# Rounding attention values on GpSimd, and one MLP tile's low parts on VectorE

## The chip, the cores and the metric

The kernel runs on one core of a Trainium2 chip. The metric is the device time of one execution in microseconds (us); before the change the median of three runs is 1063.71 us. A core has TensorE (PE in the rows, its weight loads are PEld), VectorE (DVE), ScalarE (ACT), GpSimd (POOL) and SyncE (SP), which issues the DMAs. Each engine works through its own list of instructions in order and waits on semaphores for the others.

## The reference, cut to what matters

Causal attention with an added memory read-out, and then two MLPs, one after the other, over the 2304 rows that the attention leaves:

```python
# q, k, v: 4 batches x 8 heads x 576 rows x 64
a = softmax(causal(q @ k.T / 8));  local = a @ v
mem = (phi(q) @ M_prev) / (phi(q) . z_prev + 1e-6)
x = g * mem + (1 - g) * local          # g = sigmoid(beta), per head; x: 2304 x 512
h = x @ w_in;   x = elu(h) @ w_out     # w_in 512 x 2048, w_out 2048 x 512
h = x @ w2_in;  y = max(0.01 * h, h) @ w2_out
```

The weights come as 64-bit floats, which the kernel takes apart into words and turns into float32 itself.

## The kernel before, in words

**Precision.** Most matmuls use operands of type fp32r. A float32 value is written as two such numbers: the rounded value (the high part) and the difference between the value and it (the low part). A product then takes three matmuls (high x high, low x high, high x low). Rounding is a copy into a tile of that type; the low part is a `tensor_tensor` subtract of the value and the high part.

**Attention.** The four batches are four tiles, `ti` 0 to 3. A tile has four pairs of heads (`Pair`), a pair four items (two heads, two groups of rows). Tile 0, `ti < V32` with `V32 = 1`, is computed in plain float32. From tile 1 on keys, queries, probabilities and values are split into high and low parts. `v_unit` does that for the values of a pair: two copies `vv <- vn` of 128x320 (lines 261 and 380; the rows name the helper's line, 261) on the engine `E_VH`, which is VectorE, and then two subtracts on GpSimd (line 385), which need the copies. It also rounds the memory matrices on GpSimd (`ms <- mr`). The matmuls that read `vv` (line 542) come two items later. Each item further has the scores with their row maximum on VectorE (line 449, `pt <- sc,mask`, and `mx`), the exponential on ScalarE (line 454), the scaling by the row sum on GpSimd (line 469, `pt <- pt,rs,omg`), and transposes on TensorE (line 475). `phi_unit` makes phi(q): line 405 on VectorE (`ph_f`), lines 407 and 414 on GpSimd (`ph_e`), which TensorE then transposes (line 348). The transposes of q and k are lines 357 and 312.

**MLP 1, attention's share.** As soon as a batch is done, seven of the sixteen slices of 128 hidden columns are computed for its rows in pieces of 288; these units are woven into the attention of the next batch, and fill TensorE from some 125 us on.

**MLP 1, wide tiles.** The other nine slices run afterwards over five wide tiles of 512 rows (the last has 256). The loop over `gi` (line 932) goes through slices `f` 7 to 15: twelve matmuls (`h_mm`, line 639), `elu` (lines 652 to 654: Relu and Exp on ScalarE, one combining pass on VectorE), and `g_split` (line 642), which rounds the activation on VectorE (`gh <- e`, helper line 261) and subtracts on GpSimd (`gl <- e,gh`, line 646), both 128x512; the output matmuls (line 672) read `gh` and `gl`. During the first wide tile the weights of slices 11 to 15 are still being decoded: ScalarE scales a word (line 134), VectorE shifts and merges (lines 135, 136, 139), ScalarE rounds, VectorE makes the low part (line 147, `w`). MLP 2 follows, with its own steps.

**What sets the order.** The Tile framework builds each engine's list while the kernel is compiled: units are emitted in the program's order, which gives them priorities (`tc.high_priority` moves some forward), and the framework's scheduler with a simulated timeline decides from them in which order instructions stand on each engine. Operations on tiles wait for their producers and, where a buffer is reused, for its last readers.

```python
V32 = 1
E_GH, E_WH, E_VH, E_MS, E_V32, E_XH, E_RS, E_Y = "V", "A", "V", "P", "P", "A", "P", "A"
NW, NG, EB = TW, 3, 2      # wide tiles: 512 rows, 3 buffers of gh and gl, 2 of e
```

Of the kernel before, what the change touches and what calls it, by code (L numbers as in the profile page):

```python
# [12 lines left out]
ALU = mybir.AluOpType  # L13
AX = mybir.AxisListType

P = 128
# [3 lines left out]
def _f(ap):  # L20
    return ap.bitcast(F32)
# [3 lines left out]
def kernel(  # L25
# [14 lines left out]
    nc = tc.nc  # L40
# [12 lines left out]
    V32 = 1  # L53
# [4 lines left out]
    E_GH, E_WH, E_VH, E_MS, E_V32, E_XH, E_RS, E_Y = "V", "A", "V", "P", "P", "A", "P", "A"  # L58
# [105 lines left out]
    def halves(n):  # L164
# [22 lines left out]
        out=mask[:, 448:576], in_=mask[:, 448:576], pattern=[[-1, 128]], compare_op=ALU.is_ge,  # L187
# [37 lines left out]
    def bank(tag):  # L225
        return psum.tile([P, 512], F32, tag=tag, bufs=BANKS[tag], name=tag)
# [31 lines left out]
    def copy(eng, dst, src):  # L258
        if eng == "A":
            return nc.scalar.copy(dst, src)  # L260
        return (nc.vector if eng == "V" else nc.gpsimd).tensor_copy(dst, src)  # L261
# [8 lines left out]
    class Pair:  # L270
# [94 lines left out]
        def v_unit(self):  # L365
            vv = at.tile([P, 1344], F32R, tag="vv", bufs=2, name="vv")
            nk = 5 if self.cb == 5 else 2
            ms = self.ms = self.pad["m32" if self.full_v else "ms"]
            if self.full_v:
                v32 = _f(vv)[:, 0:640].rearrange("p (c d) -> p c d", d=128)[:, 0:nk, :]  # L370
                copy(E_V32, v32, self.v[:, 0:nk, :])
                for c in range(nk):
                    self.vc[0, c] = self.vc[1, c] = v32[:, c, :]
                for j, ps, _ in self.heads():
                    nc.gpsimd.tensor_copy(ms[ps, j, :], self.mr[ps].rearrange("p h e -> p (h e)"))
                return
            vn = self.v.rearrange("p c (j d) -> p j c d", j=2)[:, :, 0:nk, :]
            for j in range(2):
                vh = vv[:, 704 * j:704 * j + 640].rearrange("p (c d) -> p c d", d=128)[:, 0:nk, 0:64]
                copy(E_VH, vh, vn[:, j])  # L380
            for j in range(2):
                blk = vv[:, 640 * j:640 * j + 640].rearrange("p (c d) -> p c d", d=128)
                hi = blk[:, 0:nk, 64 * j:64 * j + 64]
                lo = blk[:, 0:nk, 64 - 64 * j:128 - 64 * j]
                nc.gpsimd.tensor_tensor(
                    out=lo, in0=self.v[:, 0:nk, 64 * j:64 * j + 64], in1=_f(hi), op=ALU.subtract
                )
                for c in range(nk):
                    self.vc[j, c] = blk[:, c, :]
            for j, ps, po in self.heads():  # L390
                mh = ms[ps, j, 64 * j:64 * j + 64]
                ml = ms[ps, j, 64 - 64 * j:128 - 64 * j]
                copy(E_MS, mh, self.mr[ps, j, :])
                nc.gpsimd.tensor_tensor(out=ml, in0=self.mr[ps, j, :], in1=_f(mh), op=ALU.subtract)
# [224 lines left out]
    def mtile(tag, bufs, dt=F32, shape=None):  # L619
        shape = shape or (NW,)  # L620
        pool = pools.get(("own", tag), pools["mlp"])
        return pool.tile([P] + list(shape), dt, tag=tag, bufs=bufs, name=tag)
# [12 lines left out]
    def h_mm(ph, wi, xh, xl):  # L635
        n_mm = 0
        for kc in range(NKC):
            for wj, xx in ((0, xh), (1, xh), (0, xl)):
                nc.tensor.matmul(ph, wi[:, wj, kc, :], xx[:, kc, :], start=n_mm == 0, stop=n_mm == 11)  # L639
                n_mm += 1  # L640

    def g_split(g, w):
        gh = mtile("gh", NG, F32R)[:, 0:w]
        gl = mtile("gl", NG, F32R)[:, 0:w]
        hi = copy("A" if attending else E_GH, gh, g)
        lo = nc.gpsimd.tensor_tensor(out=gl, in0=g, in1=_f(gh), op=ALU.subtract)  # L646
        pools["elu"] = [hi.ins, lo.ins]
        return gh, gl

    def elu(ph, w):  # L650
        e = mtile("e", EB)[:, 0:w]
        nc.scalar.activation(out=e, in_=ph, func=AF.Relu, scale=-1.0)
        ex = nc.scalar.activation(out=e, in_=e, func=AF.Exp, scale=-1.0)
        nc.vector.scalar_tensor_tensor(out=e, in0=e, scalar=-1.0, in1=ph, op0=ALU.add, op1=ALU.max)
        g = g_split(e, w)
        pools["elu"].append(ex.ins)
        return g

    def leaky(ph, w):
        t = mtile("e", EB)[:, 0:w]  # L660
        sc = nc.scalar.mul(t, ph, 0.01)
        nc.vector.tensor_tensor(out=t, in0=ph, in1=t, op=ALU.max)
        g = g_split(t, w)
        pools["elu"].append(sc.ins)
        return g

    def o_mm(py, fs, key, ec, gs, first, last, opens=True, closes=True):
        for f in fs:
            wo = wo_tiles[key, f]
            gh, gl = gs[f]  # L670
            for n_mm, (wj, gg) in enumerate(((0, gh), (1, gh), (0, gl))):
                nc.tensor.matmul(  # L672
                    py, wo[:, wj, ec * P:(ec + 1) * P], gg,
                    start=opens and f == first and n_mm == 0, stop=closes and f == last and n_mm == 2,
                )

    attending = True
    tail = False
    n_ph = 0

    def h_bank():
        nonlocal n_ph
        n_ph += 1
        return bank("tp" if tail and n_ph % 2 else "pm")
# [175 lines left out]
    def load2(t0, n):  # L860
        xs = wide_x()
        for x, scr in zip(xs, xp_scr):
            recut(_f(x), scr, t0, n)
        return [x[:, :, 0:n] for x in xs]
# [65 lines left out]
    with tc.high_priority(offset=EARLY):  # L930
        cur = load2(*wide[0])
    for gi, (t0, w) in enumerate(wide):
        gs = {}
        pys = {}

        def emit_out(f):
            for ec in range(NKC):
                if f == NFA:
                    pys[ec] = bank(("sc", "sc", "sc", "po")[ec])[:, 0:w]
                o_mm(pys[ec], [f], 0, ec, gs, NFA, NF - 1)  # L940
            del gs[f]

        ys = []

        def fetch_y():
            ne = NKC * TN // w
            for e in range(NKC // ne):
                yt = mtile("yx"[e], 1, F32, (ne, w))
                for pi, (_, _, pw, tok) in enumerate(parts):
                    lo, hi = max(tok, t0), min(tok + pw, t0 + w)  # L950
                    if lo < hi:
                        nc.sync.dma_start(
                            yt[:, :, lo - t0:hi - t0], y_scr[pi][:, ne * e:ne * e + ne, lo - tok:hi - tok]
                        )
                ys.extend(yt[:, i] for i in range(ne))

        for f in range(NFA, NF):
            for _ in wun[:2 if f == NFA else 1]:
                waiting.append(wun.pop(0)[1]())
            if f == NFA + 3:  # L960
                fetch_y()
            ph = h_bank()[:, 0:w]
            h_mm(ph, wi_tiles[0, f], *cur)
            gs[f] = elu(ph, w)
            with tc.issue_after(pools["elu"][2]):
                if merged:
                    merged.pop()()
                if waiting:
                    merged.append(waiting.pop(0)())
            if f > NFA + 1:  # L970
                emit_out(f - 2)
            if gi >= 1 and f - NFA in (W2A, W2B) and len(w2) > NF - NFA:
                w2.pop(0)()
        emit_out(NF - 2)
        if gi + 1 < len(wide):
            cur = load2(*wide[gi + 1])
        emit_out(NF - 1)
        for ec in range(NKC):
            x1 = ys[ec]
            nc.vector.tensor_tensor(out=x1, in0=pys[ec], in1=x1, op=ALU.add)  # L980
            nc.sync.dma_start(x1_scr[gi][:, ec], x1)
# [209 lines left out]
```

## Time and profile before

| what | value |
|---|---|
| runs before | 1063.42, 1063.71, 1064.23 us |
| the profiled execution, its own time | 1064.19 us |
| its span, first to last instruction | 1062.2 us |
| mean granted clock of TensorE | 0.994 |
| TensorE busy | 1035.5 us, 97% |
| VectorE busy | 700.6 us, 66% |
| ScalarE busy | 512.3 us, 48% |
| GpSimd busy | 514.1 us, 48% |
| chain that ended last | TensorE 89%, VectorE 5% |

All times in rows are microseconds from the start of the span unless marked ns. Busy time says how long an engine had an instruction in it; a wait in brackets behind a timeline row, as `[1.06 <-DVE mx L449]`, is how long the engine sat idle before that row and which instruction released it. The granted clock is the share of TensorE's full speed that was allowed: 1.00 is 2.4 GHz and 0.50 is 1.2 GHz. In shapes, 128x320 is partitions x elements.

### The profile page before, as it was taken

To read this page: it belongs to the slowest core of one execution; us is meant where nothing else is said; L and a number is where in the kernel's file an instruction comes from. 1 tells how busy PE (TensorE), PEld (TensorE's weight loads), DVE (VectorE), ACT (ScalarE), POOL (GpSimd) and SP (SyncE) were. 2 spreads that over 40 slices of the span, in tenths; PEclk is the share of its full clock that TensorE was granted. 3 is DMA by queue.
4 is the path that set the end of the run, shared out by engine and by line. 5 is a ranking of instruction groups with operands and counts; after the bars stand their busy time and mean duration, and the time that the engine had idled before them with its cause. 6 is when DMAs were issued, how large, how long until landed. Compare 5 with 4: busy or idle time off the path is not lost.

```text
span 1062.2 us, 18157 instructions
## 1 busy us (share of the span) xinstructions
PE 1035.5 (97%) x6192; PEld 918.9 (87%) x6192; DVE 700.6 (66%) x1547; ACT 512.3 (48%) x1219; POOL 514.1 (48%) x642
## 2 busy tenths in 40 slices
PE   6998899999999999999999999999999999999998
PEld 3776799989998999978888889888888899899897
DVE  6889987888889746597762324754599755564532
ACT  5999887787878735544442224422122222322211
POOL 7665785677667725434443225764233122222321
PEclk9999999999999999999999999999999999999999
DMA  7754543564456239476572303430152543352110
GB/s 183 196 152 111 161 135 101 138 172 139 106 139 169 85 92 345 163 229 212 184 237 81 119 1 124 154 110 10 56 222 119 198 159 119 120 179 80 40 40 21
DMA packets 151708, 143.41 MB, mean 135 GB/s; under 512 B 80448, under 2 KB 137792, under 8 KB 148544
## 3 DMA queue, kind: packets, MB, share of 16 engines
q1 hardware_dynamic: 151472, 142.00, 43.6%
q8 instruction: 49, 0.80, 0.3%
q14 instruction: 43, 0.35, 0.1%
q10 hardware_dynamic: 144, 0.26, 0.1%
HBM read 97.39 MB, written 41.29 MB: 131 GB/s over the span
## 4 chain that ended last, share of the span: by engine, by line
PE 89%; DVE 5%; DMA 1%; ACT 1%; SPq 1%; issue 1%; POOL 1%; DVEq 0%; ACTq 0%
PE pm L639 17%; PE sc L1049 14%; PE tp L639 12%; PE sc L672 10%; PE pm L672 5%; PE po L1049 4%; PE tp L475 4%; PE po L542 4%; PE pm L1067 4%; PE tp L1067 4%; PE po L672 2%; PE pm L542 2%; PE sc L446 2%; PE sc L447 2%; PE sc L444 1%
## 5 line engine op out<-in xcount | busy, mean ns | idle before, releaser
L646 POOL TENSOR_TENSOR gl<-e,gh 128x512 fp32r<-128x512 f32 (+2 forms) x149 | 167.2, 1125 | 287.9 <-DVE gh L261 173.3
L1049 PE MATMUL sc<-w,gh 128*128 128x512 f32 x448 | 135.2, 392 | 0.0
L469 POOL TENSOR_SCALAR pt<-pt,rs,omg 128x128 f32<-128x128 f32 (+4 forms) x160 | 103.3, 655 | 20.4 <-DVE rs L464 16.2
L639 PE MATMUL tp<-xw,w 128*128 128x512 f32 (+1 forms) x376 | 104.9, 360 | 0.7 <-DVE w L147 0.7
L454 ACT ACTIVATE pt<-pt,mx 128x128 f32<-128x128 f32 (+4 forms) x160 | 93.4, 585 | 23.2 <-DVE mx L449 21.6
L672 PE MATMUL sc<-gh,w 128*128 128x512 f32 (+2 forms) x438 | 103.4, 341 | 0.1
L639 PE MATMUL pm<-xw,w 128*128 128x512 f32 (+1 forms) x368 | 102.9, 361 | 0.0
L1079 POOL TENSOR_TENSOR gl<-e,gh 128x512 fp32r<-128x512 f32 x32 | 41.4, 1295 | 122.6 <-ACT gh L1078 93.7
L1049 PEld LDWEIGHTS sc<-w,gh 128*128 128x128 f32 x448 | 80.6, 189 | 13.6
L475 PE MATMUL tp<-ident,pt 128*128 128x128 f32 x480 | 83.4, 280 | 3.4 <-DVE al L268 1.5
L1049 PE MATMUL sc<-w,gl 128*128 128x512 f32 x224 | 82.9, 390 | 0.0
L672 PEld LDWEIGHTS sc<-gh,w 128*128 128x128 f32 x438 | 74.4, 188 | 9.8 <-DVE gh L261 1.4
L639 PE MATMUL pm<-xh,w 128*128 128x288 f32 x368 | 80.1, 304 | 1.6 <-ACT xh L628 1.6
L639 PEld LDWEIGHTS tp<-xw,w 128*128 128x128 f32 x376 | 67.8, 189 | 12.3 <-DVE w L147 1.1
L639 PEld LDWEIGHTS pm<-xw,w 128*128 128x128 f32 x368 | 66.3, 189 | 11.1
L449 DVE CUSTOM_DVE_ANT_0 pt<-sc,mask 128x128 f32<-128x128 f32 (+4 forms) x160 | 69.4, 445 | 7.5 <-PE sc L447 3.5
L475 PEld LDWEIGHTS tp<-ident,pt 128*128 128x128 f32 x480 | 59.7, 143 | 10.0 <-ACT ah L265 2.4
L639 PE MATMUL tp<-xv,w 128*128 128x512 f32 (+1 forms) x188 | 67.7, 360 | 0.0
L672 PE MATMUL sc<-gl,w 128*128 128x512 f32 (+2 forms) x219 | 66.5, 341 | 0.2 <-POOL gl L646 0.2
L639 PE MATMUL pm<-xv,w 128*128 128x512 f32 (+1 forms) x184 | 66.5, 361 | 0.0
L149 POOL TENSOR_TENSOR w<-wm,w 128x512 fp32r<-128x512 f32 x40 | 52.6, 1336 | 26.1 <-ACT w L260 26.1
L672 PE MATMUL pm<-gh,w 128*128 128x288 f32 x280 | 63.3, 306 | 0.0
(214 smaller groups left out, 2684.4 us busy)
## 6 DMA issues: line engine op xcount, KB each, us to landing
wraw<-in_moe_w_in_dram SPq DMA_DIRECT2D x32, 512.0 KB, 4.0
wraw<-in_moe_w_out_dram SPq DMA_DIRECT2D x32, 512.0 KB, 5.0
wraw<-ws SPq DMA_DIRECT2D x16, 1024.0 KB, 4.9
ws<-wraw SPq DMA_DIRECT2D x8, 1024.0 KB, 3.8
xh<-xh SPq DMA_DIRECT2D x8, 576.0 KB, 3.4
xl<-xl SPq DMA_DIRECT2D x8, 576.0 KB, 3.8
ys<-st SPq DMA_DIRECT2D x32, 144.0 KB, 2.9
vn<-in_v_dram SPq DMA_DIRECT2D x64, 64.0 KB, 2.3
```

The costliest lines, as they stand in the source:

```text
L149: nc.gpsimd.tensor_tensor(out=w[:, 1, a], in0=t[:, a], in1=_f(w)[:, 0, a], op=ALU.subtract)
L449: nc.vector.tensor_tensor_reduce(out=pt[0:m, k0:k0 + n], in0=sc[0:m, 0:n], in1=mk, op0=ALU.add, op1=ALU.min, scale=-0.125, scalar=mx[0:m, ...
L454: nc.scalar.activation(out=pt[0:m, 0:nk], in_=pt[0:m, 0:nk], func=AF.Exp, scale=-1.0, bias=mx[0:m, last:last + 1], accum_out=self.pd["ss"] ...
L469: nc.gpsimd.tensor_scalar(out=pt, in0=pt, scalar1=rs[0:m, i:i + 1], scalar2=omg[0:m, h:h + 1], op0=ALU.mult, op1=ALU.mult,)
L475: nc.tensor.transpose(dst, self.p[c][:, k0:k0 + kn], ident)
L542: nc.tensor.matmul(po[:, a:b], w, x, start=i == 0, stop=i == len(mms) - 1)
L639: nc.tensor.matmul(ph, wi[:, wj, kc, :], xx[:, kc, :], start=n_mm == 0, stop=n_mm == 11)
L646: lo = nc.gpsimd.tensor_tensor(out=gl, in0=g, in1=_f(gh), op=ALU.subtract)
L672: nc.tensor.matmul(py, wo[:, wj, ec * P:(ec + 1) * P], gg, start=opens and f == first and n_mm == 0, stop=closes and f == last and n_mm == 2,)
L1049: nc.tensor.matmul(pos[tb], gg[:, tb * P:(tb + 1) * P], wo[:, wj, :], start=f == 0 and n_mm == 0, stop=f == NF - 1 and n_mm == 2,)
L1067: nc.tensor.matmul(out, wb[:, a, kc, :], xb[b][:, kc, :], start=kc == n == 0, stop=kc == 1 and n == 2)
L1079: nc.gpsimd.tensor_tensor(out=gl, in0=flat, in1=_f(gh), op=ALU.subtract)
```

## The change

For the first tile behind the float32 part (`ti == V32`, that is tile 1) the two rounding copies `vv <- vn` of each pair go to GpSimd; tiles 2 and 3 keep them on VectorE. And in the first wide tile of MLP 1 (`gi == 0`) the low part `gl` of each activation is subtracted by VectorE; everywhere else GpSimd goes on doing that. A flag, `lows_on_vector`, says which.

```diff
-                copy(E_VH, vh, vn[:, j])
+                copy("P" if self.ti == V32 else E_VH, vh, vn[:, j])
...
-        lo = nc.gpsimd.tensor_tensor(out=gl, in0=g, in1=_f(gh), op=ALU.subtract)
+        lo = (nc.vector if lows_on_vector else nc.gpsimd).tensor_tensor(out=gl, in0=g, in1=_f(gh), op=ALU.subtract)
...
+    lows_on_vector = False
...
     for gi, (t0, w) in enumerate(wide):
+        lows_on_vector = gi == 0
```

## Rows read from the trace of the kernel before

**Rows 1.** The page's busy time by engine, share of the span, instructions.
```profile
PE 1035.5 (97%) x6192; PEld 918.9 (87%) x6192; DVE 700.6 (66%) x1547; ACT 512.3 (48%) x1219; POOL 514.1 (48%) x642
```

**Rows 2.** Windows: stretch, length, busy of PE, PEld, DVE, ACT, POOL; clock, DMA.
```profile
80.00:96.00 16.00, 15.12 (x85) 11.44 (x84) 15.31 (x44) 14.56 (x42) 8.43 (x13) 1.00 0.44 98
96.00:106.00 10.00, 7.85 (x46) 6.29 (x44) 9.15 (x26) 9.19 (x26) 6.93 (x13) 0.83 0.50 136
119.00:126.00 7.00, 5.14 (x27) 4.21 (x27) 6.78 (x19) 5.13 (x15) 5.44 (x9) 0.76 0.46 113
126.00:210.00 84.00, 84.00 (x660) 83.67 (x659) 69.10 (x208) 67.09 (x192) 57.20 (x91) 1.00 0.52 140
453.00:500.00 47.00, 45.95 (x198) 36.45 (x197) 40.40 (x46) 21.59 (x28) 20.36 (x12) 1.00 0.69 224
```

**Rows 3.** Timeline of TensorE at its waits near 100 and 121 us.
```profile
99.78 0.41 PE L446 MATMUL sc<-kk,qs 128*128 128x288 f32 x1 [1.06 <-DVE mx L449]
100.94 0.44 PE L357 MATMUL sc<-ident,qn 128*128 128x128 f32 x2 [0.51 <-DVE mx L449]
...
120.78 0.44 PE L348 MATMUL po<-ident,ph_e 128*128 128x128 f32 x2 [1.27 <-POOL ph_e L414]
121.82 1.01 PE L357 MATMUL sc<-ident,qn 128*128 128x128 f32 x3 [0.60 <-DVE mx L449]
```

**Rows 4.** Timeline of VectorE: the rounding copies of three pairs of tile 1.
```profile
79.35 0.72 DVE L261 CAST vv<-vn 128x320 fp32r<-128x320 f32 x2
...
97.26 2.10 DVE L261 CAST vv<-vn 128x320 fp32r<-128x320 f32 x2
...
119.18 1.76 DVE L261 CAST vv<-vn 128x320 fp32r<-128x320 f32 x2
```

**Rows 5.** Timeline of GpSimd beside the second and third of those.
```profile
96.93 2.21 POOL L469 TENSOR_SCALAR pt<-pt,rs,omg 64x320 f32<-64x320 f32 x3 [0.86 <-PE pm L542]
...
119.47 1.26 POOL L414 TENSOR_TENSOR ph_e<-ph_f,den 128x640 f32<-128x640 f32 x1
```

**Rows 6.** GpSimd's copies and subtracts by source line: ns min/median/max, first and last start.
```profile
L261 POOL CAST ms<-mr x24: 227/236/243, 58.5 to 342.4; 64x64 fp32r<-64x64 f32 x24
L261 POOL COPY vv<-vn x4: 717/717/718, 13.1 to 61.3; 128x640 f32<-128x640 f32 x4
L385 POOL TENSOR_TENSOR vv<-vn,vv x24: 856/872/927, 80.2 to 345.4; 128x320 fp32r<-128x320 f32 x24
```

**Rows 7.** Line 405 on VectorE by source line; GpSimd and VectorE near 81 us.
```profile
L405 DVE SCALAR_TENSOR_TENSOR ph_f<-qn,ph_e x16: 805/826/1406, 9.1 to 355.9; 128x640 f32<-128x640 f32 x16
...
80.25 1.68 POOL L385 TENSOR_TENSOR vv<-vn,vv 128x320 fp32r<-128x320 f32 x2
...
81.21 1.41 DVE L405 SCALAR_TENSOR_TENSOR ph_f<-qn,ph_e 128x640 f32<-128x640 f32 x1 [0.16 <-ACT ph_e L404]
```

**Rows 8.** Timeline of VectorE, first wide tile: weight decode, 128x1024 each.
```profile
455.35 1.72 DVE L136 SCALAR_TENSOR_TENSOR wm<-wraw,wm 128x1024 int32<-128x1024 int32 x1
...
459.67 1.72 DVE L136 SCALAR_TENSOR_TENSOR w<-wraw,w 128x1024 int32<-128x1024 int32 x1
...
462.78 2.32 DVE L139 SCALAR_TENSOR_TENSOR w<-wraw,w 128x1024 int32<-128x1024 int32 x1
...
473.45 2.20 DVE L136 SCALAR_TENSOR_TENSOR w<-wraw,w 128x1024 int32<-128x1024 int32 x1
...
476.71 1.21 DVE L139 SCALAR_TENSOR_TENSOR w<-wraw,w 128x1024 int32<-128x1024 int32 x1
...
479.92 1.99 DVE L147 TENSOR_TENSOR w<-w,w 128x1024 fp32r<-128x1024 f32 x1 [0.25 <-ACT w L260]
```

**Rows 9.** Waits of TensorE from 453 to 500 us: total, times, longest.
```profile
PE tp L639 <- DVE w L147: 0.7, 1, 0.7
PE sc L672 <- POOL gl L646: 0.2, 1, 0.2
```

**Rows 10.** A 128x512 operation of VectorE with two SBUF inputs, by source line.
```profile
L868 DVE TENSOR_TENSOR xw<-y,xw x4: 678/682/1024, 837.1 to 923.2; 128x512 fp32r<-128x512 f32 x4
```

## The prediction

> **What bounds the kernel now.** I read the page's busy times first: TensorE is busy for 1035.5 of 1062.2 us [rows 1]. Any gain has to come out of the 27 us in which it waits, or out of stretches with a lower clock. So the next view is the table of windows, laid over the two places that the change touches. Where the values of tile 1 are rounded, from 80 to 126 us, VectorE is the engine that is full: 15.31 of 16, 9.15 of 10 and 6.78 of 7 us, while TensorE has 0.88, 2.15 and 1.86 us free in the same three windows and its clock falls to a mean of 0.83 in the second and 0.76 in the third. From 126 to 210 us the seven-slice units have begun, TensorE is busy in all 84.00 us, and whatever was saved before moves through undiminished [rows 2]. The first wide tile is another matter: from 453 to 500 us TensorE is busy in 45.95 of 47 us, so at most 1.05 us can be had there, with VectorE at 40.40 [rows 2]. Third, the timelines. TensorE waits 1.06 and 0.51 us near 100 us and 0.60 us at 121.8, each time for a row maximum of VectorE, and 1.27 us at 120.8 for GpSimd's `ph_e` [rows 3]. VectorE's timeline shows what it does ahead of those maxima: the two copies `vv <- vn` of a pair, which take 0.72 us at 79.35, but 2.10 us at 97.26 and 1.76 us at 119.18 [rows 4]. Beside the long ones GpSimd runs its own work, three scalings of 2.21 us in all, and the 1.26 us of `ph_e` [rows 5]. One of the long pairs thus ends just before TensorE's 1.06 us wait ends, and the other before its 0.60 us wait.
>
> **Part one, the copies.** Eight copies leave VectorE, two for each of four pairs, and eight come to GpSimd. No DMA is moved, and nothing is removed from TensorE or ScalarE. GpSimd's own subtracts (line 385) no longer wait for VectorE, since the copy is ahead of them on the same engine.
>
> The trace shows no 128x320 copy with rounding on GpSimd. From below: a 64x64 one takes 236 ns and a 128x640 copy without rounding 717; the line through both gives 236 + 256 x 0.835 = 450 ns at 320 elements. From above: the two-input subtract of the same shape takes 872 ns [rows 6]. I take 0.45 us, as the rows of one-input copies are nearest; that is 0.9 us for a pair (1.74 at the upper end). GpSimd has the room on average (8.43 of 16, 6.93 of 10, 5.44 of 7 us [rows 2]), so I cost it at nothing; that cover is gone where a copy stands ahead of something that TensorE is waiting for, which is the slower rival below.
>
> What comes back, pair by pair:
> - First pair, 79.35: VectorE has the copies for 0.72 us [rows 4]. Its next long step, `ph_f`, waits for ScalarE (0.16 us) and then takes 1.41 us beside GpSimd's subtracts, where the median of its sixteen is 0.83 [rows 7]. VectorE is not quite what limits here, so I take 0.3 us back. Bounds: 0.72 us gained, or 0.58 us lost (1.41 - 0.83), if GpSimd's longer queue holds up `ph_f` for as long again.
> - Second pair, 97.26: without the 2.10 us, the maximum comes as early as its scores let it, and the 1.06 us wait closes. The 0.51 us wait behind it, for the other half of the same maximum, stays. I take 1.06 us; the bounds are nothing, if the wait only gets another name, and 2.10 us.
> - Third pair, 119.18: the 0.60 us wait closes. The 1.27 us ahead of it belongs to GpSimd's `ph_e` and is late next: it stays. 0.60 us, between nothing and 1.76.
> - Fourth pair: its copies fall in the window from 126 us, where TensorE has no free time [rows 2]. Nothing, either way.
> - The clock. Behind each of the two waits TensorE runs at 1.2 GHz for a while; by the means of the windows 10 x 0.17 + 7 x 0.24 = 3.4 us of full-speed time are lost [rows 2]. VectorE was nearly full in those stretches as well, so a faster TensorE would only have waited more for it. With the copies gone that is no longer so: 2.10 + 1.76 = 3.86 us of VectorE's work are gone, of which 1.66 are counted above; the other 2.2 us can only be had if TensorE keeps up. I take not quite half, 1.0 us; bounds 0 and 3.4.
>
> **Part two, the low parts.** Nine subtracts of 128x512 go to VectorE. That operation isn't in the rows on VectorE; another of its subtracts of this size with both inputs in SBUF has a median of 0.68 us [rows 10]. Some eight fall in the window from 453 to 500 us: 5.4 us more on an engine with 6.6 us free there. But GpSimd does hardly anything else in that stretch, and its subtracts stand beside VectorE's slow decode steps: five of them take 1.72, 1.72, 2.32, 2.20 and 1.99 us, where the same shape takes 1.21 alone [rows 8]; 9.95 - 5 x 1.21 = 3.9 us of stretching. If GpSimd is silent, this goes. The Trainium skill says the same (SBUF — State Buffer, "Who interferes with whom"): GpSimd and VectorE share one pair of ports under an exclusive lock, a VectorE instruction with two SBUF inputs and a GpSimd one that reads SBUF keep each other out, and the later waits to the end of the earlier. By that rule all of the 3.9 us goes, and the sum below stands; without it part two would cost 3.4 us.
>
> On the path there is just one thing: TensorE's 0.7 us wait for the weights of a decoded slice, and 0.2 us for `gl` [rows 9]. Ahead of that wait VectorE gets five subtracts, 5 x 0.68 = 3.4 us, and loses 0.51 + 0.51 + 1.11 + 0.99 = 3.1 us of stretching: 0.3 us later. The 0.2 us for `gl` goes. Net 0.1 us slower; bounds 1.05 us gained (all the free time of that window) and 3.4 us lost (no stretching goes).
>
> **The sum.** -0.3 - 1.06 - 0.60 - 1.0 + 0.1 = -2.9 us (rounded). The profiled execution took 1064.19 us, with 2.0 us around its span of 1062.2, and would come to 1061.3. It lies 0.5 us above the median of the runs, 1063.71; from that median the forecast is 1060.8 us.
>
> **The rivals.**
> - GpSimd becomes late (slower). Place: GpSimd's queue between 79 and 126 us, three pairs. If the scheduler puts the copies ahead of the scalings of line 469 or of `ph_e`, these come later by the copies, and TensorE's transposes with them. At the price of the two-input subtract, 2 x 0.87 x 3 = 5.2 us, against 1.96 us gained at the three waits: +3.2, or 1066.9 us. It decides once the copies start while TensorE's next transposes are already waiting for GpSimd. For it: the 1.27 us wait is one for GpSimd already [rows 3]. Against it: the free shares above, and the lower price is nearer.
> - The copies hold up VectorE from the other side (no change). A GpSimd instruction beside `ph_f` makes it 1.41 instead of 0.83 us [rows 7]. If the new copies do so at three pairs, 3 x 0.58 = 1.7 us go back, and with the clock not regained the sum is -1.96 + 1.7 + 0.1 = -0.1: 1063.6 us. For it: `ph_f` follows the copies closely in the first pair. Against it: the engines meet only if their orders bring them together. The Trainium skill's lock (SBUF — State Buffer, "Who interferes with whom") would work just this way, since copies on GpSimd read SBUF too, and so speaks against part one.
> - VectorE becomes the bound in the wide tile (no change). The stretching stays, through the transfers or ScalarE, and the weights come 3.4 us later: -2.96 + 3.4 - 0.2 = +0.2, or 1063.9 us. For it: VectorE is at 40.40 of 47 us. Against it: five stretched steps with GpSimd beside them.
> - More comes back than at the waits (faster). All of 0.72 + 2.10 + 1.76 = 4.6 us of VectorE's time, and half of the clock's 3.4: -6.3, or 1057.4 us. For it: VectorE is at 95% there. Against it: TensorE has waits on ScalarE and GpSimd as well.
> - That the change does less than it says cannot be with the copies (the condition picks tile 1). But the order on every engine is made anew by the scheduler's simulation, so small waits may come or go far from both edits; this widens every case by perhaps 1 us.
>
> **How the numbers follow.** Forecast 0.44, its own range 1058.9 to 1062.7; GpSimd late 0.16; VectorE held up 0.14; wide tile bound 0.13; more comes back 0.13. A measurement of this kernel can tell about 0.2% from no change, 2.1 us: below 1061.6 is faster, above 1065.8 slower. Of the forecast's 0.44, 0.40 lie below 1061.6 (its upper end, with the clock not regained, doesn't). Faster: 0.40 + 0.13 = 0.53. Same: 0.04 + 0.14 + 0.13 = 0.31. Slower: 0.16. The range goes from 1057.2 to 1065.6 us: it leaves out most of the slower case and a part of the fastest, less than 2 in 10.
>
> **What would show it.** Right: between 97 and 101 us VectorE has no `vv <- vn`, TensorE's wait of 1.06 us is gone, and the window's clock is above 0.83; GpSimd has eight copies of some 0.45 us; in the first wide tile no decode step takes over 1.3 us, `gl` takes 0.68 us on VectorE, and TensorE's wait for `w` is within 0.5 us of 0.7. Wrong: copies of 0.8 us or more on GpSimd, TensorE waiting for `pt` or `ph_e` between 80 and 126 us for longer than now, a `ph_f` of 1.4 us in each pair, or new waits for `w` near 476 us. If TensorE's free time between 80 and 126 us is as before and the time falls all the same, my account of it is wrong.

## The result: slower, and the profile after

The changed kernel takes 1079.49 us (median of 4 runs, 1076.99 to 1080.48), the kernel before 1063.74 in the same session: a ratio of 1.0144, 95% interval 1.0131 to 1.0156. That is 15.8 us slower, where 1060.8 us was forecast and 1065.6 was the upper end of the range.

The profiled execution took 1079.98 us, with a span of 1078.2 where it was 1062.2. First the page's line of busy times, which answers to [rows 1]:

```profile
PE 1042.5 (97%) x6192; PEld 922.5 (86%) x6192; DVE 701.7 (65%) x1548; ACT 512.5 (48%) x1219; POOL 499.2 (46%) x641
```

TensorE has the same 6192 instructions. It is busy 7.0 us longer, though it does the same work, and it idles 35.7 us (1078.2 less 1042.5) where it idled 26.7. The windows that answer to [rows 2], in the same columns:

```profile
80.00:96.00 16.00, 14.26 (x79) 10.61 (x78) 14.97 (x39) 13.81 (x38) 8.88 (x14) 1.00 0.44 98
96.00:106.00 10.00, 8.59 (x49) 7.18 (x47) 7.72 (x27) 9.38 (x27) 6.71 (x13) 0.83 0.50 122
119.00:126.00 7.00, 6.05 (x42) 4.58 (x40) 6.70 (x20) 6.14 (x18) 6.53 (x14) 1.00 0.46 119
126.00:210.00 84.00, 82.66 (x633) 82.04 (x634) 66.29 (x194) 65.60 (x185) 55.13 (x88) 0.98 0.49 133
453.00:500.00 47.00, 43.69 (x204) 35.33 (x203) 33.36 (x45) 19.66 (x25) 5.58 (x5) 1.00 0.60 198
```

Between 80 and 126 us little is gained: TensorE is free for 4.1 us in the first three windows where it was for 4.9, the second has the clock that it had (0.83), and the waits for a row maximum, which were to shrink, add up to 3.4 us from 80 to 126 us where they were 2.7. From TensorE's waits in that stretch, first before and then after the change:

```profile
PE sc L446 <- DVE mx L449: 1.6, 3, 1.1
...
PE sc L357 <- DVE mx L449: 1.1, 2, 0.6
```

```profile
PE sc L446 <- DVE mx L449: 3.2, 3, 1.4
...
PE sc L357 <- DVE mx L449: 0.2, 1, 0.2
```

From 126 to 210, where TensorE had no free time, 1.3 us are now free. To see where the 16 us arise, take one matmul at each of several places and compare its start in the timelines of both executions:

| matmul on TensorE | before, us | after, us | later by |
|---|---|---|---|
| 161st transpose of line 475 | 123.3 | 123.8 | 0.6 |
| 241st transpose of line 475 | 191.6 | 195.2 | 3.6 |
| 241st of line 639, pieces of 288 rows | 243.8 | 253.9 | 10.1 |
| 421st of the same | 370.9 | 381.0 | 10.2 |
| first of the first wide tile | 437.9 | 451.7 | 13.9 |
| 145th of the wide tiles | 504.0 | 520.3 | 16.4 |
| end | 1062.2 | 1078.2 | 16.0 |

The largest step, 6.5 us, falls between 195 and 254 us. There tile 1 ends and tile 2 begins, and neither edit touches that work. TensorE's waits in that place after the change (engine, tile and line, what it waited for: total, times, longest):

```profile
PE pm L639 <- ACT xh L628: 1.9, 1, 1.9
PE sc L357 <- DVE mx L449: 0.7, 1, 0.7
PE tp L475 <- DVE dl L268: 0.5, 1, 0.5
PE po L542 <- DVE xp L549: 0.4, 1, 0.4
PE sc L357 <- DVE kl L320: 0.4, 1, 0.4
```

Before, the same place had two:

```profile
PE tp L475 <- DVE al L268: 1.2, 1, 1.2
PE sc L357 <- DVE kl L320: 0.8, 1, 0.8
```

In both kernels TensorE has run out of woven-in MLP units there (in the timelines from 213 to 222 us before, from 217 to 229 after), and lives on the attention alone. The next units need rows that VectorE adds (line 714 before, 715 after), by source line, first before and then after the change:

```profile
L714 DVE TENSOR_TENSOR x<-x,y x4: 442/444/556, 220.3 to 222.0; 128x288 f32<-128x288 f32 x4
```

```profile
L715 DVE TENSOR_TENSOR x<-x,y x4: 444/750/1925, 226.8 to 229.4; 128x288 f32<-128x288 f32 x4
```

They come 6.5 us later, and one takes 1925 ns, beside subtracts of GpSimd. Behind that gap the windows of the changed kernel show the lower clock:

```profile
217.20:229.20 12.00, 8.40 (x51) 5.99 (x49) 10.22 (x33) 10.00 (x32) 7.49 (x15) 0.97 0.32 90
228.50:235.50 7.00, 5.87 (x25) 5.51 (x26) 6.31 (x15) 4.58 (x11) 5.67 (x8) 0.51 0.72 220
```

0.51 is the 1.2 GHz level: TensorE had been busy for 8.40 of 12.00 us ahead of it. What that costs is seen below, where another kernel has the same list and the lower clock for half as long.

The moved operations, on the other hand, cost what was forecast. GpSimd's copies and subtracts by source line, which answer to [rows 6], then VectorE's new subtracts:

```profile
L261 POOL CAST vv<-vn x8: 451/454/464, 80.0 to 146.7; 128x320 fp32r<-128x320 f32 x8
...
L385 POOL TENSOR_TENSOR vv<-vn,vv x24: 854/876/929, 80.8 to 355.4; 128x320 fp32r<-128x320 f32 x24
...
L646 DVE TENSOR_TENSOR gl<-e,gh x9: 679/683/1783, 468.6 to 513.8; 128x512 fp32r<-128x512 f32 x9
```

Laid side by side in the two traces, the instruction lists of before and after are alike up to about 79 us (TensorE's up to 92). From there on every engine's list is in another order, TensorE's until 562 us. Hence two theories. **Order**: the lists that the scheduler made anew lose the time. **Work**: the moved operations lose it, where they stand or by what they hold up.

### The profile page after: what moved, and what is told of

Its sections match the earlier page's. It is cut to its first block, busy times and chain, and to the rows that moved or that the text cites. A ratio compares the mean times of both kernels' runs of the same rounds, so it can differ in the third digit from the quotient of the medians.

```text
span 1078.2 us, 18145 instructions
## 1 busy us (share of the span) xinstructions
PE 1042.5 (97%) x6192; PEld 922.5 (86%) x6192; DVE 701.7 (65%) x1548; ACT 512.5 (48%) x1219; POOL 499.2 (46%) x641
## 4 chain that ended last, share of the span: by engine, by line
PE 83%; DVE 5%; DMA 4%; ACT 3%; issue 2%; SPq 1%; POOL 0%; DVEq 0%; ACTq 0%; POOLq 0%
PE pm L639 15%; PE sc L1051 14%; PE tp L639 11%; PE sc L672 8%; PE pm L672 5%; PE po L542 4%; PE po L1051 4%; PE tp L475 4%; PE pm L1069 4%; PE tp L1069 4%; PE pm L542 2%; PE po L672 2%; PE sc L446 2%; PE sc L447 2%; DMA wraw<-in_moe_w_out_dram 1%
## 5 line engine op out<-in xcount | busy, mean ns | idle before, releaser
L646 POOL TENSOR_TENSOR gl<-e,gh 128x512 fp32r<-128x512 f32 (+2 forms) x140 | 153.2, 1096 | 274.4 <-DVE gh L261 157.4
L469 POOL TENSOR_SCALAR pt<-pt,rs,omg 128x128 f32<-128x128 f32 (+4 forms) x160 | 100.6, 638 | 19.3 <-DVE rs L464 18.1
L454 ACT ACTIVATE pt<-pt,mx 128x576 f32<-128x576 f32 (+4 forms) x160 | 93.0, 583 | 20.1 <-DVE mx L449 19.1
L149 POOL TENSOR_TENSOR w<-wm,w 128x512 fp32r<-128x512 f32 x40 | 52.0, 1321 | 59.4 <-ACT w L260 55.1
L639 PEld LDWEIGHTS pm<-xh,w 128*128 128x128 f32 x368 | 60.4, 193 | 3.2 <-ACT xh L628 3.1
```

The costliest lines, as they stand in the source:

```text
L149: nc.gpsimd.tensor_tensor(out=w[:, 1, a], in0=t[:, a], in1=_f(w)[:, 0, a], op=ALU.subtract)
L454: nc.scalar.activation(out=pt[0:m, 0:nk], in_=pt[0:m, 0:nk], func=AF.Exp, scale=-1.0, bias=mx[0:m, last:last + 1], accum_out=self.pd["ss"] ...
L469: nc.gpsimd.tensor_scalar(out=pt, in0=pt, scalar1=rs[0:m, i:i + 1], scalar2=omg[0:m, h:h + 1], op0=ALU.mult, op1=ALU.mult,)
L646: lo = (nc.vector if lows_on_vector else nc.gpsimd).tensor_tensor(out=gl, in0=g, in1=_f(gh), op=ALU.subtract)
```

## The experiments

### Work and order taken apart

A kernel can be held to a recorded order. Neighbours on an engine are tied by an edge that costs no semaphore; an instruction that changes its engine stands on the new one where it stood in the order of all instructions.

```diff
         tile_attn_moe_kernel(tc, *args)
+        _hold_order(tc)
...
+    for n in order:
+        i = traced[n]
+        e = str(i.engine)
+        if e in last:
+            tc.add_manual_dep(i, last[e].name, info, reason="hold_order")
+        last[e] = i
```

**both_oldorder** has both edits and the order of before; **none_neworder** has no edit and the order of the changed kernel. Their traces show the lists that were meant: in all 6192 places TensorE has the same matmul as in before, or as in the changed kernel.

> Both edits, but each engine's list is held in the order that it had before the change; a moved instruction stands on its new engine where it stood in the order of all instructions. Theory O: the loss goes away, and what my prediction summed for the operations alone is left: 1058 to 1064 us, about 1061. Theory W: the operations are the same as in the changed kernel, so the time is too: 1077 to 1080 us.

> No edit, every operation on the engine that it had before; each engine's list is held in the order that the changed kernel has. Theory O: about the time of the changed kernel, 1075 to 1082 us. Theory W: about the time of before, 1062 to 1066 us.

Measured: 1062.01 us (0.9985, interval 0.9976 to 0.9995) and 1080.34 us (1.0153, 1.0137 to 1.0168), against 1063.85 for before. With the result this fills a square:

| | order of before | order of the changed kernel |
|---|---|---|
| work of before | 1063.85 | 1080.34 |
| both edits | 1062.01 | 1079.49 |

The order costs 16.5 us without the edits and 17.5 with them. The edits themselves gain 1.8 us in the order of before; the 0.9 us of the other column is not clear of noise, since the intervals 1.0131 to 1.0156 and 1.0137 to 1.0168 overlap. The order theory holds, in both directions. The kernel with no edit has the same late place, by the waits of TensorE from 205 to 245 us:

```profile
PE pm L639 <- ACT xh L628: 1.9, 1, 1.9
PE sc L357 <- DVE kl L320: 0.9, 1, 0.9
PE sc L357 <- DVE mx L449: 0.7, 1, 0.7
```

and the window behind them, with the clock between its two levels on average:

```profile
228.00:236.00 8.00, 6.80 (x41) 6.55 (x41) 7.13 (x18) 5.85 (x15) 5.43 (x7) 0.79 0.74 224
```

This prices the lower clock. By these means (8 us at 0.79 here, 7 us at 0.51 in the changed kernel) TensorE is at 1.2 GHz for half as long here, with the same list. The 80 matmuls from 225.3 us on in the changed kernel, and from 224.3 us on here, take 16.5 and 16.1 us. So the other half, some 3.5 us at 1.2 GHz, costs 0.4 us, not half of its length. Even if the first half did cost that, 1.7 us (an estimate), no more than 2.1 of the 6.5 us would be the clock's.

### One edit at a time, in an order of its own

**copies** is the first hunk of the diff alone, **lows** the other three.

> The copies of tile 1 on GpSimd alone; the low parts of the first wide tile stay on GpSimd, and the order is made freely. Theory O (the order): the loss comes from the new lists that the scheduler makes from about 77 us on, and most of it lies before 440 us, where only the copies can have caused it. Then about 1077 us (1063.7 + 13.9, the shift of the first wide tile in the changed kernel), with the same two late places near 230 and 426 us, and between 1075 and 1079. Theory W (the work): the moved copies cost at their own place, between 80 and 126 us, by keeping GpSimd and VectorE apart; then this too is slower, by about 3 us where they stand, and the rest of the loss has to come from the low parts: about 1066 to 1068 us.

> The low parts of the first wide tile on VectorE alone; the copies stay on VectorE. The first 430 us have the order of before. Theory O: what the wide tile loses is the 2.5 us that the changed kernel loses there, and nothing before it: 1063.7 to 1066.5 us. Theory W: VectorE's nine subtracts and the weights that come later behind them carry most of the loss: 1070 us or more.

Measured: 1077.04 us (1.0133, 1.0113 to 1.0154) and 1066.35 us (1.0022, 1.0012 to 1.0031). Both lie in the range of the order theory: the copies carry 13 us. For the low parts this run cannot tell order from work; the next can.

### One edit at a time, in the order of before

> Only the copies are moved, each engine's list held as before. My sum for the operations gave -3.0 us; both edits in the old order measured -1.6 us (interval -2.6 to -0.5). Theory O with the copies as the gain: 1061 to 1062.5 us. If the copies gain nothing at their own place: 1063 to 1064.5. Theory W (the moved work costs): above 1065.

> Only the low parts are moved, each engine's list held as before. My sum gave +0.1 us for this edit, with bounds of -1.05 and +3.4. Theory O: the +2.3 us of the same edit in its own order go away: 1062.5 to 1064 us. If VectorE's nine subtracts themselves make the weights late: 1065.5 to 1067.

Measured: 1062.58 us (0.9991, 0.9982 to 1.0) and 1063.04 us (0.9989, 0.9979 to 0.9999). The low parts lose nothing where the order stays. The copies gain 1.1 us, just short of the range for a gain (1061 to 1062.5), with an interval that reaches no change. TensorE's waits in the wide tile, from 436 to 505 us, of **lows**:

```profile
PE pm L639 <- ACT w L260: 2.5, 2, 1.3
PE tp L639 <- ACT w L260: 0.7, 1, 0.7
PE sc L672 <- DVE gl L646: 0.2, 1, 0.2
```

and of **lows_oldorder**:

```profile
PE sc L672 <- DVE gl L646: 1.4, 1, 1.4
```

The same subtracts on the same engine: in the new list the decoded weights come late three times, in the old one only `gl` does, once.

### How little it takes

**copies_pair3** moves only the two copies of tile 1's last pair.

```diff
-                copy(E_VH, vh, vn[:, j])
+                copy("P" if self.ti == V32 and self.hp in (3,) else E_VH, vh, vn[:, j])
```

> Only two of the eight copies move, those of the last pair of tile 1, which fall in the stretch from 126 us where TensorE has no free time; the order is made freely. For these two my sum had nothing, either way. Theory O: the lists are made anew from there on, so that the time moves all the same, by more than 2 us from 1063.8, to either side, with nothing different before 126 us. Theory W: 1062.5 to 1065 us.

Measured: 1075.83 us (1.0117, 1.0102 to 1.0133). Two copies of 449 ns, in a stretch where TensorE waits for nothing, and 12 us are lost. The two next kernels move nothing; they set one column, which is overwritten later, to zero:

```diff
             vn = self.v.rearrange("p c (j d) -> p j c d", j=2)[:, :, 0:nk, :]
+            if self.ti == V32 and self.hp == 3:
+                nc.vector.memset(_f(vv)[:, 640:641], 0.0)
```

with `nc.gpsimd` for `nc.vector` in **one_column_pool**.

> Nothing moves. VectorE sets one column of the value tile (128x1, overwritten later) to zero, once, ahead of the two copies of the last pair of tile 1; the order is made freely. Its own cost is that of a 128x1 operation, which I put at 0.1 us on an engine that is not the bound there. Theory O: any small change on VectorE has the lists made anew behind it; then the time moves by several us, as it did for the two copies of this pair: 1070 to 1078 us, with the late places near 228 and 420 us. Rival: it takes the change of engine; then 1063 to 1065 us.

> The same one column at the same place, set to zero by GpSimd, whose list has room there: the lists of TensorE, VectorE and ScalarE come out as before. Theory O: 1063 to 1065 us, as before. If the operation or the extra dependency of the value tile is what costs: the same as with VectorE.

Measured: 1074.02 us (1.0092, 1.0079 to 1.0106) and 1063.45 us (0.9998, 0.9989 to 1.0007). The added instruction of **one_column** by source line:

```profile
L379 DVE MEMSET vv<- x1: 59/59/59, 143.6 to 143.6; 128x1 f32 x1
```

and TensorE's longest waits from 217 to 264 us (its lines stand two further down: 641 is 639 of before):

```profile
PE sc L448 <- DVE qs L361: 1.6, 2, 1.4
PE pm L641 <- ACT xh L630: 1.5, 1, 1.5
PE tp L477 <- POOL pt L471: 0.6, 1, 0.6
```

59 ns of work cost 10 us, and not where they stand: by the timelines this kernel is 0.2 us behind before at the 241st transpose (191.6 us of before), 48 us behind the column, and 9.9 us at the first wide tile. On GpSimd the same column takes 127 ns and costs nothing. There the lists of TensorE, VectorE and ScalarE come out as before; with VectorE at least 1528 of TensorE's 6192 places, a quarter, hold another matmul by the traces. The rival, that a change of engine is needed, falls.

### What the new lists lack

**late_fill** is the changed kernel in its own order but for the last two output units of tile 0, A and B (21 matmuls each). In terms of TensorE's list, by the times of the changed kernel:

```diff
-207.3 A x21
-211.8 to 217.1 B x21
+218.2 A x4, 218.9 A x3, 219.7 A x3, 222.0 A x7, 223.2 A x4
+223.8 B x4, 224.5 B x3, 224.9 B x3, 225.6 B x3, 226.9 B x8
```

ScalarE's copies of their results (`st <- pm`) move with them.

> The changed kernel in its own order, with one difference: the last two output units of tile 0's MLP share (42 matmuls, about 5.6 us, which TensorE does from 207 to 217 us) stand later in the lists, in pieces between 217 and 229 us, where TensorE has no MLP work and waits 0.41, 0.51, 0.69, 1.87 and 0.39 us, and behind which it runs at 1.2 GHz for 6.8 us. If it is the want of filler there that loses the time: between 3.5 us (the waits alone) and 7 us (the clock as well) come back, 1072 to 1076 us. If the loss has another cause there, the waits only move: 1078 to 1080.

Measured: 1076.54 us (1.0124, 1.011 to 1.0137), between the two ranges expected. That is 3.0 us less than the changed kernel's 1079.49, but the intervals of the two ratios overlap, so the total alone does not show a gain. The place shows one: from the 241st transpose to the 241st matmul of line 639, the step of 6.5 us in the table above, this kernel's profile has 55.1 us, the changed kernel's 58.7, that of **none_neworder** 57.9 and that of before 52.2. So 2.8 to 3.6 of the 6.5 us come back, less than I expected. Its windows:

```profile
217.00:229.00 12.00, 10.29 (x81) 10.02 (x80) 10.81 (x32) 9.34 (x28) 7.83 (x14) 1.00 0.33 89
228.00:236.00 8.00, 8.00 (x61) 7.37 (x60) 7.38 (x19) 7.21 (x21) 6.17 (x10) 1.00 0.76 231
```

and the one wait of TensorE between them, in its timeline:

```profile
226.62 0.67 PE L639 MATMUL pm<-xh,w 128*128 128x288 f32 x3 [1.71 <-ACT xh L628]
```

TensorE is busy for 10.29 of the 12 us, and its clock is full where the changed kernel had 0.51 (a part of the attention now runs ahead of the filler, so these windows don't hold quite the same work). The wait for the rows stays. It is not the waits that were filled: in the stretch of 55.1 us TensorE is free for 3.6 us, and for 4.0 in the changed kernel's 58.7; what came back is busy time, 3.1 us. How much of that is the clock's is not separated; a full clock is not enough, for the profile of **one_column** has it too from 217 to 236 us and takes 56.5 us for the same stretch. **early_rows** has that order and places the additions, roundings and subtracts of those rows earlier; the first addition and the first rounding, which the kernel keeps in program order, are let go for that:

```diff
-226.8 VectorE: four additions; 228.8 ScalarE: four roundings; 229.3 GpSimd: four subtracts
+217.7 VectorE: four additions, ScalarE: four roundings; 219.7 GpSimd: three subtracts
```

> The changed kernel with the late filler (the last two output units of tile 0 in pieces between 217 and 229 us), and besides with the next rows prepared earlier: the four additions, their roundings and three of the four subtracts stand some 9 us further ahead in the lists of VectorE, ScalarE and GpSimd, where VectorE and GpSimd wait. Their rows have landed by 204 us. With the late filler alone TensorE still waits 1.71 us for them at 226.6. If they are late because of their place in the lists, that wait goes: 1074 to 1075.5 us. If something else holds them: 1076 to 1077.

Measured: 1077.7 us (1.0125, 1.0112 to 1.0139). That is no gain, and above both ranges. The wait for `xh` is gone, and two others have come:

```profile
215.56 0.41 PE L542 MATMUL po<-qph,ms 128*128 128x320 f32 x1 [1.27 <-DVE xp L549]
...
228.56 0.53 PE L639 MATMUL pm<-xh,w 128*128 128x288 f32 x2 [1.12 <-ACT st L260]
```

The additions now stand ahead of VectorE's copy `xp`, which frees the bank that TensorE's next product needs. So the loss there is shown to lie in the lists, and a part of it to come back with filler; moving these rows alone brings back nothing.

### The better kernel once more

> Both edits in the order of before once more, in more rounds. One edit at a time gave 0.9991 and 0.9989. If they add up: 0.998, about 1061.6 us; if the gain is one and the same: 0.999, about 1062.7.

Measured: 1061.95 us (0.9982, 0.9973 to 0.9991). Within their intervals the two gains add up, and this version lies 1.7 us, 0.2%, below before. Its copies by source line:

```profile
L261 POOL CAST vv<-vn x8: 443/448/457, 80.3 to 143.8; 128x320 fp32r<-128x320 f32 x8
```

and three of its windows:

```profile
96.00:106.00 10.00, 7.73 (x49) 5.59 (x49) 7.93 (x28) 9.65 (x28) 8.09 (x15) 1.00 0.47 122
119.00:126.00 7.00, 4.81 (x33) 3.73 (x34) 6.21 (x19) 6.75 (x18) 6.76 (x12) 1.00 0.61 169
...
453.00:500.00 47.00, 45.58 (x200) 37.06 (x200) 42.07 (x53) 21.90 (x29) 4.14 (x3) 1.00 0.71 232
```

GpSimd has nearly left the wide tile (4.14 us for 20.36 in [rows 2]), and VectorE carries 42.07 there without holding TensorE up any more than before (45.58 busy for 45.95).

## Why the prediction was wrong, point by point

**The step that failed** is the last of the rivals: "the order on every engine is made anew by the scheduler's simulation, so small waits may come or go far from both edits; this widens every case by perhaps 1 us". The mechanism was named, and its size was given without a row behind it. It measures 16.5 to 17.5 us by the square, 10 us for one column. No rival came above 1066.9 us, and what was saved ahead of 126 us was to move through undiminished; instead the new lists give TensorE 1.3 us of free time from 126 to 210 us and lose 6.5 us from 195 to 254. All the rest of the sum rests on the lists of before; with those held, the kernel comes out at 1062.0, inside the range and 1.2 us above the forecast. Why it is not lower still is a matter of the pairs and the clock, below.

**The price of the copies** was right: 0.45 us taken, 0.454 and 0.448 measured, at the lower bound.

**The pairs** (-0.3, -1.06 and -0.60) came out smaller. With the old order (**both_oldorder_again**), TensorE's waits from 96 to 106 us are these:

```profile
PE tp L475 <- POOL pt L469: 1.0, 2, 0.8
PE po L348 <- DVE qpl L268: 0.6, 1, 0.6
PE sc L357 <- DVE kl L320: 0.4, 1, 0.4
```

The 1.06 us wait for the maximum [rows 3] is gone, as forecast, and so is the 0.51 us one, which was to stay; waits for GpSimd's scaling and for other steps of VectorE stand in their place, 2.0 us in all for 1.8. The 0.60 us wait at 121.8 is gone as well, and at 125.3 TensorE waits as long for GpSimd, whose list is longer by the copies (from its waits from 80 to 126 us):

```profile
PE pm L639 <- POOL xl L632: 0.6, 1, 0.6
```

These waits got another name, which was the lower bound of both terms. It is the slower rival, GpSimd late, at a fifth to a third of its price (1.0 us for the scaling, 1.6 with `xl`, of 5.2). I compare the three kernels with the copies on GpSimd in the old order and four that have before's lists in this stretch (before, lows, lows_oldorder, one_column_pool), by the transposes of line 475:

| transposes | pair | copies on GpSimd, us | on VectorE, us |
|---|---|---|---|
| 81st to 121st | first | 25.9 | 25.8 to 25.9 |
| to the 141st | second | 13.3 to 13.4 | 13.4 to 13.9 |
| to the 161st | third | 11.2 | 12.5 to 12.8 |
| to the 181st, with the wait for `xl` | | 18.0 | 17.2 to 17.3 |
| to the 201st | fourth | 14.9 | 14.9 |
| all | | 83.4 to 83.5 | 84.1 to 84.8 |

About 1 us comes back where -2.96 was summed with the clock: most of it at the third pair, behind which 0.7 us is lost again.

**The clock** (-1.0, bound 3.4) was a wrong term. Windows of **one_column_pool**, whose TensorE, VectorE and ScalarE have before's lists:

```profile
96.00:106.00 10.00, 7.03 (x45) 5.01 (x45) 9.15 (x24) 9.26 (x25) 7.00 (x12) 1.00 0.53 136
119.00:126.00 7.00, 4.57 (x29) 2.98 (x28) 6.78 (x19) 5.46 (x15) 5.50 (x9) 1.00 0.46 116
```

The clock is full where [rows 2] had 0.83 and 0.76, and TensorE is merely idle for longer: that execution needs 84.4 us for the same 120 transposes, the one of before 84.6. VectorE is as full in both (9.15 and 6.78 us), and the difference of 0.2 us is smaller than that among the four executions. The forecast said as much for VectorE with the copies, and wanted the clock back without them; but there it is worth no more. The profile of **both_oldorder** has a clock of 0.83 from 96 to 106 us, that of **both_oldorder_again** 1.00, and the 120 transposes take 83.5 and 83.4 us. The bound took the product of window and missing clock for time lost.

**The low parts** (+0.1) came out well. Each takes 0.68 us, as [rows 10] had it, and the stretched decode steps [rows 8] are gone: in **lows_oldorder** and **both_oldorder_again** every step of lines 136, 139 and 147 from 440 to 530 us takes 1.21 to 1.23 us, as do these of the changed kernel:

```profile
469.81 1.22 DVE L136 SCALAR_TENSOR_TENSOR wm<-wraw,wm 128x1024 int32<-128x1024 int32 x1
472.48 1.21 DVE L139 SCALAR_TENSOR_TENSOR wm<-wraw,wm 128x1024 int32<-128x1024 int32 x1
473.62 1.22 DVE L136 SCALAR_TENSOR_TENSOR w<-wraw,w 128x1024 int32<-128x1024 int32 x1
```

The rule of the Trainium skill that I weighed there (SBUF — State Buffer, "Who interferes with whom") agrees with these rows; so does the one low part that took 1.78 us, at 513.75 us, beside a subtract of GpSimd that ran from 513.41 for 1.58 us. The waits came out the other way round: the one for `w` (0.7 us) is gone, where it was to come 0.3 us later, and the one for `gl`, which was to go, is 1.4 us long in the old order. In the old order the stretch from the first to the 145th matmul of the wide tiles is 0.5 us shorter than before (65.6 for 66.1), in the new one 2.5 us longer (68.6); in **none_neworder**, with the low parts still on GpSimd, it takes 69.1. The loss there, too, is the order's.

**What stays open**: why the scheduler's choice comes out worse each time it is disturbed at this spot, by two copies, by eight or by a column. I did not try its settings (the lead of the woven-in units and their delay) with both edits in, which would be the way without a recorded order. The steps of 3.0 us from 124 to 195 us and of 3.7 between 381 and 452 in the table of places are the order's (the kernel with no edit has 2.3 and 4.1 there), but were not traced to single waits.

## What to carry to other kernels

Where a framework's scheduler makes the instruction lists, an edit is two changes, of the work and of every list behind it, and the second can be ten times the first; price the order by what a neutral disturbance does, not by a guess. Hold the old order and put the edit into it, and hold the new order with the edit taken out: these two runs say which of the two changes you have measured. Where the order is to stay free, an edit on an engine with slack can leave the other lists as they are, as the one column on GpSimd did; that is one case and no rule, for two copies moved to that engine did not.

## What the runs showed of the hardware that was not expected

Executions of the same lists differ in where TensorE falls to 1.2 GHz: from 80 to 126 us twice in the profiles of before and **lows_oldorder**, once in that of **lows**, never in that of **one_column_pool**. The time for the stretch does not follow it: 84.6, 84.8, 84.1 and 84.4 us for the 120 transposes. Where another engine limits, or TensorE stands waiting, a low clock in a profile need not be time lost. And a 128x288 addition of VectorE with both inputs in SBUF took 1.93 us instead of 0.44 in the changed kernel while GpSimd ran two 128x320 subtracts, 1.68 us in all (226.74 to 228.42 in its timeline). That fits the lock on shared ports (the Trainium skill, SBUF — State Buffer, the section named above), but no run was made to take the two apart.
